# The last token tile's output columns cut 512 and 128 instead of 320 and 320, with a store for each part

## Chip, cores and metric

The kernel runs on one core of one Trainium2 chip. The metric is the device time of one execution in microseconds; the median of several executions is given, lower is better. Times inside an execution come from a hardware profile of one execution and are counted from the start of its span.

## What is computed

Input x has 2048 tokens of 640 channels in bf16. The output is the sum of x itself, a sliding-window attention on the layer-normalised x, and a gated bilinear unit on the same normalised x:

```
xn  = layernorm(x)
qkv = xn @ wqkv                                  # 32 heads of 20 channels
attn over 8 keys per token, 2 tokens apart       # masked at the start
a   = (attention output) @ wo
h   = (xn @ w_gate) * (xn @ w_up)                # 1536 wide
out = x + a + h @ w_down
```

The last line is the part that matters here. For 128 tokens and a group of output columns, `h @ w_down` (12 matmuls over the 1536 channels of h) and `o @ wo` (5 matmuls over the 640 channels of the attention output) are accumulated in the same PSUM bank, and x is added when the bank is read.

## The kernel before

The 2048 tokens are 16 tiles of 128 (`NT`), in 4 chunks of 4 tiles (`CH`). For each chunk the kernel runs the attention (`prodlog`, `softmax`, `av`: mostly VectorE, with short matmuls at line 484), the gated unit (`glu`: 24 groups of five 512-column matmuls at line 610, copied out by ScalarE at line 615 and multiplied by VectorE at line 626 into `hT`), then `down` for each of its four tiles, and between these the layer norm, transposes and projections of a later chunk (`ln`, `transposes`, `qk`, `vproj`). The last chunk has no later chunk beside it, so the end of the kernel is `glu` of chunk 3 and then `down(12)` to `down(15)`.

`down(t)` does the last line of the reference for one tile. `load_xr` fetches the tile of x into `xr` (a DMA on GpSimd's queue, long before). The 640 output columns are cut into two parts `n` of `NS` = 320 columns. For each part `pe` issues 12 matmuls of line 648 (weights: a 128x128 block of `hT`; moving: 320 columns of `wd`) and 5 of line 651 (weights: a block of the transposed attention output `oT`; moving: 320 columns of `wo`), all into one PSUM bank. `evict` then adds `xr` to the bank on VectorE (line 657) and writes the sum back into the same columns of `xr`. When both parts are done, `st` stores all 640 columns of the tile with one DMA (line 679): on GpSimd's queue for tiles 0 to 13, on SyncE's queue (SP) for tiles 14 and 15. For the first tile of a chunk (`q == 0`) the matmuls come in another order; tile 15 has `q == 3` and takes the plain branch.

The order of all instructions is made ahead of time by a planner (`Plan`). Every step is added with its engine, an estimated cost, how long it occupies the engine (`occ`), and the steps it depends on. `order` works out for each step the latest time at which it may start, counted back from the end over its successors' costs, and then runs through time: on each engine, of the steps that are ready, the one with the earliest such time goes first. The estimates decide the order only; on the chip each instruction starts when its engine and its semaphores allow. TensorE's main steps are chained by `pe_main`, which also lets a step wait for the eviction of the bank used six groups earlier (`ring`). Estimates that are used by `down` are 0.136 us for a matmul of 320 columns, 0.486 for an eviction and 2.3 for a store.

At the end of the program (line 794) SP waits for the semaphores of all DMAs and engines, two to an instruction, before the engines meet in a barrier.

Of the kernel before, what the change touches and what calls it, by code (L numbers as in the profile page):

```python
# [10 lines left out]
ALU = mybir.AluOpType  # L11
# [20 lines left out]
class Plan:  # L32
# [8 lines left out]
    def add(self, eng, cost, fn, deps=(), occ=None, after=(), kb=0):  # L41
        s = Step(eng, cost, fn, deps, occ, after)
        s.kb = kb
        s.idx = len(self.steps)
        self.steps.append(s)
        return s
# [51 lines left out]
def kernel(  # L98
# [11 lines left out]
    nc = tc.nc  # L110
    P = nc.NUM_PARTITIONS
    x_flat = A_x.flatten_outer_dims()
    out_flat = out.flatten_outer_dims()
    S, D = x_flat.shape
# [8 lines left out]
    KT = D // P  # L123
    FT = F // P
    NT = S // P
# [4 lines left out]
    NS = D // 2  # L130
# [12 lines left out]
    wo = const.tile([P, KT, D], BF, name="wo")  # L143
    wg = const.tile([P, KT, F], BF, name="wg")
    wu = const.tile([P, KT, F], BF, name="wu")
    wd = const.tile([P, FT, D], BF, name="wd")
# [7 lines left out]
    add = plan.add  # L154
    T = {}

    def new(key, shape, dtype, tag, bufs, pool=None):
        t = (pool or sb).tile(shape, dtype, name=tag, tag=tag, bufs=bufs)
        T[key] = t
        return t  # L160
# [127 lines left out]
    def st_in(t, g, d=None):  # L288
        return inline("DVE", 0.48, ln_stats(t, g), [d or X[t]], 0.395)
# [19 lines left out]
    def pe_main(cost, fn, deps=(), banks=1):  # L309
        nonlocal main  # L310
        waits = []
        for k in range(banks):
            if len(ring) + k >= 6:
                waits.append(ring[len(ring) + k - 6])
        main = add("PE", cost + 0.165, fn, [main, *waits, *deps], occ=cost)
        return main
# [313 lines left out]
    XR, OB = {}, {}  # L630

    def load_xr(t):
        def fn():
            x = new(("xr", t), [P, D], BF, "xr", 4)
            nc.gpsimd.dma_start(out=x[:], in_=x_flat[t * P : (t + 1) * P, :])
        XR[t] = add("POOL", 2.6, fn, [OB.get(t - 4), VS[6]], occ=0.5, after=[HT[t // CH, 3 + t % CH]])

    def down(t):
        c, q = divmod(t, CH)
        load_xr(t)  # L640
        evs = []
        def pe(n, f0, f1, wo_part):
            if f0 == 0:
                new(("psD", t, n), [P, 512], F32, "ps", 6, psum)
            ps = T["psD", t, n]
            sl = slice(n * NS, (n + 1) * NS)
            for f in range(f0, f1):
                nc.tensor.matmul(ps[:, 0:NS], lhsT=T["hT", c, f][:, q * P : (q + 1) * P], rhs=wd[:, f, sl],  # L648
                                 start=(f == 0), stop=(f == FT - 1 and not wo_part))
            for g in range(KT if wo_part else 0):  # L650
                nc.tensor.matmul(ps[:, 0:NS], lhsT=T["oT", t][:, g, :], rhs=wo[:, g, sl],  # L651
                                 start=False, stop=(g == KT - 1 and f1 == FT))

        def evict(n, a):
            def ev():
                sl = slice(n * NS, (n + 1) * NS)
                nc.vector.tensor_tensor(T["xr", t][:, sl], T["psD", t, n][:, 0:NS], T["xr", t][:, sl], ALU.add)  # L657
            e = add("DVE", 0.486, ev, [a, XR[t]], occ=0.4)
            ring.append(e)
            evs.append(e)  # L660

        hs = [HT[c, f] for f in range(FT)]
        W2 = [OE[t], WL["d"], WL["o"]]
        if q == 0:
            cut = FT - 2
            for n in range(2):
                pe_main((cut + KT) * 0.136, lambda n=n: pe(n, 0, cut, True), [*hs[:cut], *W2], banks=n + 1)
            ends = [pe_main(2 * 0.136, lambda n=n: pe(n, cut, FT, False), hs[cut:], banks=0) for n in range(2)]
            for n in range(2):
                evict(n, ends[n])  # L670
            a = ends[1]
        else:
            for n in range(2):
                a = pe_main((FT + KT) * 0.136, lambda n=n: pe(n, 0, FT, True), [*hs, *W2])
                evict(n, a)
        DT[t] = a

        def st():
            (nc.sync if t >= NT - 2 else nc.gpsimd).dma_start(out=out_flat[t * P : (t + 1) * P, :], in_=T["xr", t][:])  # L679

        OB[t] = add("SP" if t >= NT - 2 else "POOL", 2.3, st, evs, occ=0.5)


    a = st_in(0, 0)
    a = st_in(0, 1, a)
# [5 lines left out]
    a = st_in(1, 0)  # L691
    a = st_in(1, 1, a)
# [7 lines left out]
    a = st_in(2, 0)  # L700
    apply_in(1)
    transposes(1)
    a = st_in(2, 1, a)
# [3 lines left out]
    a = st_in(3, 0)  # L707
    a = st_in(3, 1, a)
# [48 lines left out]
    for c in range(NCH):  # L757
        attention(c)
        glu(c)
        between(c + 2, lambda q: down(c * CH + q))  # L760
        if c + 2 < NCH:
            halo(c + 2)
            qk(c + 2, 0, CS)
            for q in range(CH):
                vproj((c + 2) * CH + q)
# [33 lines left out]
```

## Time and profile before

| | |
|---|---|
| median of 3 runs | 267.35 us (267.27 to 267.51) |
| the profiled execution | 267.32 us, its span 265.6 us |
| TensorE clock granted, mean | 0.998 |
| matmuls of line 648 (320 columns) | 384, 57.4 us busy, 300 ns each |
| matmuls of line 651 (320 columns) | 160, 27.0 us busy, 299 ns each |
| matmuls of line 610 (512 columns) | 480, 119.4 us busy, 380 ns each |
| evictions of line 657 | 32, 14.8 us busy |
| stores of line 679, GpSimd's queue | 14 of 160 KB, 2.2 us from issue to landing |
| stores of line 679, SP's queue | 2 of 160 KB, 1.8 us from issue to landing |

The span runs from the first instruction to the last; the execution's own time is 1.7 us longer. Matmuls overlap each other in the array, so a matmul of 300 ns can follow another after 136 ns: the distance from start to start, not the duration, sets how long a row of them takes. "PEld" is the loading of weights, which runs beside the matmuls. "SPq" is SyncE's instruction queue, which issues DMAs. In a group's row, the number behind the bar is the busy time, then the mean duration, then the idle time of the engine before these instructions.

### The profile page before, as it was taken

The numbers are of one execution on the slowest core, as the hardware profiler recorded it, in microseconds if no ns is written. First come the engines' busy times: TensorE is split into PE (matmuls) and PEld (weight loads), VectorE is DVE, ScalarE is ACT, GpSimd is POOL, SyncE is SP. The second block draws the span as 40 slices with busy tenths as digits, with TensorE's granted clock in tenths as the row PEclk, the third lists the DMA queues.
The fourth block names the chain that finished last, engine by engine and source line by source line (L and its number), as shares of the span: only waits on it lengthen the run. The fifth ranks groups of instructions, "written<-read, shape, count | busy, mean of one in ns | idle before, by whom it ended". The sixth has DMA issues, their size and how long they took to land.

```text
span 265.6 us, 4131 instructions
## 1 busy us (share of the span) xinstructions
PE 260.1 (98%) x1594; PEld 141.5 (53%) x1594; DVE 215.5 (81%) x338; ACT 108.2 (41%) x200; POOL 40.7 (15%) x84
## 2 busy tenths in 40 slices
PE   7999999999999999999999999999999999999994
PEld 2645455444577546444466754644447764445772
DVE  5784999999999999999992999999829999921221
ACT  2666564655400166555510135555552005554000
POOL 4641025200021311400000100420000113000000
PEclk9999999999999999999999999999999999999999
DMA  7999998957496391993136937594129279110001
GB/s 224 375 406 390 368 205 263 295 137 222 113 239 144 74 367 59 299 307 32 25 71 97 334 136 222 144 288 41 20 71 346 67 230 151 25 25 0 27 33 41
DMA packets 47875, 45.89 MB, mean 173 GB/s; under 512 B 21954, under 2 KB 45008, under 8 KB 47856
## 3 DMA queue, kind: packets, MB, share of 16 engines
q1 hardware_dynamic: 43440, 35.95, 48.4%
q0 software_dynamic: 2384, 8.05, 9.7%
q10 hardware_dynamic: 2032, 1.64, 1.9%
q8 instruction: 12, 0.20, 0.4%
q14 instruction: 7, 0.06, 0.1%
HBM read 35.39 MB, written 5.26 MB: 153 GB/s over the span
## 4 chain that ended last, share of the span: by engine, by line
PE 95%; DVE 2%; DMA 1%; issue 0%
PE ps L610 39%; PE ps L648 20%; PE ps L403 16%; PE ps L651 8%; PE ps L436 7%; PE pl L484 4%; DVE st L251 1%; DMA x<-in_A_x_dram 1%; PE ps L345 0%; PE ps L331 0%; DVE x L270 0%; DVE xr L657 0%; DVE mv L257 0%; DVE ve L259 0%; DVE xnT L351 0%
## 5 line engine op out<-in xcount | busy, mean ns | idle before, releaser
L610 PE MATMUL ps<-xnT,wg 128*128 128x512 bf16 x240 | 59.7, 380 | 0.0
L610 PE MATMUL ps<-xnT,wu 128*128 128x512 bf16 x240 | 59.7, 380 | 0.0
L648 PE MATMUL ps<-wd,hT 128*128 128x320 bf16 x384 | 57.4, 300 | 0.0
L474 DVE TENSOR_TENSOR pw<-q,k 128x2560 bf16<-128x2560 bf16 x32 | 46.4, 1486 | 3.2 <-ACT k L410 3.0
L648 PEld LDWEIGHTS <-hT 128*128 128x128 bf16 x384 | 37.4, 98 | 15.9 <-issue 0.8
L571 DVE TENSOR_TENSOR v<-v,a 128x5120 bf16<-128x5120 bf16 x16 | 45.1, 2818 | 0.1
L615 ACT CAST gs<-ps 128x512 bf16<-128x512 f32 x48 | 28.1, 585 | 40.2 <-PE ps L610 40.2
L610 PEld LDWEIGHTS <-wu 128*128 128x128 bf16 x240 | 23.3, 98 | 28.7 <-issue 0.8
L610 PEld LDWEIGHTS <-wg 128*128 128x128 bf16 x240 | 23.3, 98 | 28.1 <-issue 0.8
L615 ACT CAST us<-ps 128x512 bf16<-128x512 f32 x48 | 28.1, 585 | 23.3 <-PE ps L610 22.3
L626 DVE TENSOR_TENSOR hT<-gs,us 128x512 bf16<-128x512 bf16 x48 | 19.8, 420 | 14.4 <-ACT us L615 14.3
L657 DVE TENSOR_TENSOR xr<-ps,xr 128x320 bf16<-128x320 f32 x32 | 14.8, 486 | 19.4 <-PE ps L651 15.6
L651 PE MATMUL ps<-wo,oT 128*128 128x320 bf16 x160 | 27.0, 299 | 0.0
L679 POOL DMA_DIRECT2D out_dram<-xr x14 | 7.6, 546 | 122.7 <-DVE xr L657 122.7
L580 DVE TENSOR_TENSOR v<-v 128x2560 bf16<-128x2560 bf16 x16 | 23.8, 1485 | 0.1
L436 PE MATMUL ps<-wv,xnT 128*128 128x320 bf16 x160 | 23.2, 300 | 0.4 <-ACT xnT L351 0.4
L403 PE MATMUL ps<-xnT,wk 128*128 128x512 bf16 x100 | 22.4, 380 | 0.0
L403 PE MATMUL ps<-xnT,wq 128*128 128x512 bf16 x100 | 22.2, 379 | 0.0
L436 PEld LDWEIGHTS <-xnT 128*128 128x128 bf16 x160 | 15.2, 98 | 7.2 <-ACT xnT L351 0.5
L651 PEld LDWEIGHTS <-oT 128*128 128x128 bf16 x160 | 15.6, 98 | 6.1
L410 ACT CAST q<-ps 128x512 bf16<-128x512 f32 x20 | 11.7, 585 | 16.7 <-PE ps L403 16.7
L497 ACT CAST L<-pl 128x512 bf16<-128x512 f32 x8 | 4.7, 585 | 29.2 <-PE pl L484 26.4
(58 smaller groups left out, 193.1 us busy)
## 6 DMA issues: line engine op xcount, KB each, us to landing
v<-vD SPq DMA_DIRECT2D x16, 1280.0 KB, 7.0
vD<-v_t POOLq DMA_DIRECT2D x16, 160.0 KB, 4.6
xr<-in_A_x_dram POOLq DMA_DIRECT2D x16, 160.0 KB, 5.9
out_dram<-xr POOLq DMA_DIRECT2D x14, 160.0 KB, 2.2
wg<-in_B_w_gate_dram SPq DMA_DIRECT2D x1, 1920.0 KB, 11.2
wu<-in_B_w_up_dram SPq DMA_DIRECT2D x1, 1920.0 KB, 16.5
wd<-in_B_w_down_dram SPq DMA_DIRECT2D x1, 1920.0 KB, 22.0
x<-in_A_x_dram SPq DMA_DIRECT2D x8, 160.0 KB, 4.5
```

What stands on the lines that cost most here:

```text
L403: nc.tensor.matmul(T[key][:, 0:n], lhsT=(wk if r else wq)[:, i, j * P : (j + 1) * P], rhs=T["xnT", c][:, i, lo : lo + n], start=(i == 0), ...
L410: nc.scalar.copy(dst, T[key][:, 0:n])
L436: nc.tensor.matmul(T["psv", t, n][:, 0:NS], lhsT=T["xnT", c][:, i, q * P : (q + 1) * P], rhs=wv[:, i, n * NS : (n + 1) * NS], start=(i == ...
L474: nc.vector.tensor_tensor(p[:], T["q", c][:], T["k", c][:, :, DIL * i : DIL * i + CS], ALU.mult)
L571: nc.vector.tensor_tensor(v[:].rearrange("p w (j h) -> p w j h", j=Dh, h=H), v[:].rearrange("p w (j h) -> p w j h", j=Dh, h=H), T["a", n][ ...
L580: nc.vector.tensor_tensor(v[:, 0:4, :], v[:, 0:4, :], v[:, 4:8, :], ALU.add)
L610: nc.tensor.matmul(ps[:], lhsT=(wu if r else wg)[:, i, f * P : (f + 1) * P], rhs=T["xnT", c][:, i, :], start=(i == 0), stop=(i == KT - 1))
L615: nc.scalar.copy(s[:], T[key][:])
L626: nc.vector.tensor_tensor(h[:], T["gs", c, f][:], T["us", c, f][:], ALU.mult)
L648: nc.tensor.matmul(ps[:, 0:NS], lhsT=T["hT", c, f][:, q * P : (q + 1) * P], rhs=wd[:, f, sl], start=(f == 0), stop=(f == FT - 1 and not wo ...
L651: nc.tensor.matmul(ps[:, 0:NS], lhsT=T["oT", t][:, g, :], rhs=wo[:, g, sl], start=False, stop=(g == KT - 1 and f1 == FT))
L657: nc.vector.tensor_tensor(T["xr", t][:, sl], T["psD", t, n][:, 0:NS], T["xr", t][:, sl], ALU.add)
```

## The change

For tile 15 alone the two parts are of 512 and 128 columns, and each part gets its own store on SP's queue as soon as its own eviction is done. The other tiles keep two parts of 320 and their one store. The estimates for matmuls and evictions are now formulas of the width, and these apply to all tiles; for 320 columns they come out slightly above the old constants. The old single estimate of 2.3 us for the store becomes 2.1 for each of the two.

```diff
+        last = t == NT - 1
+        at = [0, 512, D] if last else [0, NS, D]
+
         def pe(n, f0, f1, wo_part):
             if f0 == 0:
                 new(("psD", t, n), [P, 512], F32, "ps", 6, psum)
-            ps = T["psD", t, n]
-            sl = slice(n * NS, (n + 1) * NS)
+            sl = slice(at[n], at[n + 1])
+            ps = T["psD", t, n][:, 0 : at[n + 1] - at[n]]
             for f in range(f0, f1):
-                nc.tensor.matmul(ps[:, 0:NS], lhsT=T["hT", c, f][:, q * P : (q + 1) * P], rhs=wd[:, f, sl],
+                nc.tensor.matmul(ps, lhsT=T["hT", c, f][:, q * P : (q + 1) * P], rhs=wd[:, f, sl],
                                  start=(f == 0), stop=(f == FT - 1 and not wo_part))
             for g in range(KT if wo_part else 0):
-                nc.tensor.matmul(ps[:, 0:NS], lhsT=T["oT", t][:, g, :], rhs=wo[:, g, sl],
+                nc.tensor.matmul(ps, lhsT=T["oT", t][:, g, :], rhs=wo[:, g, sl],
                                  start=False, stop=(g == KT - 1 and f1 == FT))
 
         def evict(n, a):
             def ev():
-                sl = slice(n * NS, (n + 1) * NS)
-                nc.vector.tensor_tensor(T["xr", t][:, sl], T["psD", t, n][:, 0:NS], T["xr", t][:, sl], ALU.add)
-            e = add("DVE", 0.486, ev, [a, XR[t]], occ=0.4)
+                w = at[n + 1] - at[n]
+                sl = slice(at[n], at[n + 1])
+                nc.vector.tensor_tensor(T["xr", t][:, sl], T["psD", t, n][:, 0:w], T["xr", t][:, sl], ALU.add)
+            cost = 0.153 + (at[n + 1] - at[n]) / 960
+            e = add("DVE", cost, ev, [a, XR[t]], occ=cost - 0.08)
             ring.append(e)
             evs.append(e)
...
             for n in range(2):
-                a = pe_main((FT + KT) * 0.136, lambda n=n: pe(n, 0, FT, True), [*hs, *W2])
+                a = pe_main((FT + KT) * ((at[n + 1] - at[n]) / 2400 + 0.003), lambda n=n: pe(n, 0, FT, True), [*hs, *W2])
                 evict(n, a)
         DT[t] = a
 
-        def st():
-            (nc.sync if t >= NT - 2 else nc.gpsimd).dma_start(out=out_flat[t * P : (t + 1) * P, :], in_=T["xr", t][:])
-
-        OB[t] = add("SP" if t >= NT - 2 else "POOL", 2.3, st, evs, occ=0.5)
+        def st(lo=0, hi=D):
+            e = nc.sync if t >= NT - 2 else nc.gpsimd
+            e.dma_start(out=out_flat[t * P : (t + 1) * P, lo:hi], in_=T["xr", t][:, lo:hi])
+
+        if last:
+            for n in range(2):
+                add("SP", 2.1, lambda n=n: st(at[n], at[n + 1]), [evs[n]], occ=0.5)
+        else:
+            OB[t] = add("SP" if t >= NT - 2 else "POOL", 2.3, st, evs, occ=0.5)
```

## The prediction

> **What bounds the kernel now.** I read the page's totals first, then the chain that ended last, then the timeline and short windows of the last 6 us.
>
> ```profile
> span 265.6 us, 4131 instructions
> PE 260.1 (98%) x1594; PEld 141.5 (53%) x1594; DVE 215.5 (81%) x338; ACT 108.2 (41%) x200; POOL 40.7 (15%) x84
> ...
> PE 95%; DVE 2%; DMA 1%; issue 0%
> ```
>
> TensorE is busy for 98% of the span and holds 95% of the chain. So a change at the last tile can act in two ways only: through TensorE's own time, or through what follows TensorE's last matmul and has no cover. The end of the timeline shows the second:
>
> ```profile
> 259.50 1.79 PE L648 MATMUL ps<-wd,hT 128*128 128x320 bf16 x12
> ...
> 261.13 0.84 PE L651 MATMUL ps<-wo,oT 128*128 128x320 bf16 x5
> 262.01 0.49 DVE L657 TENSOR_TENSOR xr<-ps,xr 128x320 bf16<-128x320 f32 x1 [1.82 <-PE ps L651]
> 262.53 0.35 SPq L679 DMA_DIRECT2D out_dram<-xr  x1
> ```
>
> The last matmul ends at 261.13+0.84 = 261.97. The second eviction runs from 262.01 to 262.50, and the one store is issued at 262.53. The windows behind it (length, busy time of five engines, clock, DMA share, GB/s) split the rest:
>
> ```profile
> 262.53:263.38 0.85, 0.00 (x0) 0.00 (x0) 0.00 (x0) 0.00 (x0) 0.00 (x0) 1.00 0.00 0
> 263.38:263.98 0.60, 0.00 (x0) 0.00 (x0) 0.00 (x0) 0.00 (x0) 0.00 (x0) 1.00 0.77 273
> 263.98:264.34 0.36, 0.00 (x0) 0.00 (x0) 0.00 (x0) 0.00 (x0) 0.00 (x0) 1.00 0.00 0
> 264.34:265.60 1.26, 0.00 (x0) 0.00 (x0) 0.00 (x0) 0.00 (x0) 0.00 (x0) 0.61 0.00 0
> ```
>
> 0.85 us from issue to the first packet, 0.60 of packets, 0.36 until the landing releases SP, and 1.26 of closing work. The uncovered tail is 265.60-261.97 = 3.63 us, and of it only the eviction (0.49), the packets (0.60) and a little of the closing depend on how the tile is cut.
>
> **TensorE's part.** Removed: 34 matmuls of 320 columns; added: 17 of 512 and 17 of 128. Pitches (start to start): 320 columns, 1.63/12 = 0.136 us in the chain's rows of L648; 512 columns, 25.90/120 = 0.2158 in the chain's L610 row. For 128 columns the trace has the transposes of line 331, which load a new 128x128 weight for every matmul as lines 648 and 651 do:
>
> ```profile
> 17.27 0.72 PE L331 MATMUL ps<-ident,x 128*128 128x128 bf16 x10
> ```
>
> ```profile
> 17.06 0.76 PEld L331 LDWEIGHTS <-x 128*128 128x128 bf16 x10
> ```
>
> One such matmul takes 0.22, so ten of them have a pitch of (0.72-0.22)/9 = 0.0556, and their weight loads keep the pace though each lasts 98 ns: two are in flight. Tile 15 starts its first matmul at 259.50-17x0.136 = 257.19. After: the second part starts at 257.19+17x0.2158 = 260.86, its last matmul at 260.86+16x0.0556 = 261.75, and ends 0.22 later at 261.97. Before it was 261.97. TensorE gains nothing and loses nothing. Both ends for the pitch: 0.0556 (from the row) and 0.098 (loads strictly one after another), which is 17x0.042 = +0.72; a load and then the 0.056 stream behind it would be 0.154, +1.67. I take the row, since it is the same form of instruction.
>
> The Trainium skill speaks against this: "TensorE: Matmul & The Clock Gate", section Back-to-back issue gap, gives about 81 ns per matmul for sustained pairs of weight load and 128-column matmul. The trace's ten in a row ran at 56 ns. By the page's figure the second part would cost 17x0.025 = 0.43 us more, an estimate of about 267.2 for the whole.
>
> **Evictions.** These rows (busy us, mean ns) price the three widths:
>
> ```profile
> L657 DVE TENSOR_TENSOR xr<-ps,xr 128x320 bf16<-128x320 f32 x32 | 14.8, 486 | 19.4 <-PE ps L651 15.6 <-PE ps L648 3.8
> ...
> L541 DVE TENSOR_TENSOR a<-d,s 128x512 bf16<-128x512 f32 x8 | 5.5, 692 | 0.3
> ...
> L537 DVE TENSOR_TENSOR s<-s 128x128 f32<-128x128 f32 x8 | 2.3, 292 | 0.3
> ```
>
> The first eviction grows from 0.49 to 0.69. Its last matmul starts at 257.19+16x0.2158 = 260.64 and ends 0.38 later at 261.02, so it runs from 261.06 to 261.75, under the second part's matmuls (end 261.97): free, with 0.26 to spare before VectorE is wanted at 262.01. Were the second part's cover gone, it would cost up to 0.69. The second eviction shrinks from 0.49 to 0.29: 262.01 to 262.30, **-0.20** on the path. Bounds: 0.168 for the 14-column add on PSUM at line 496 and 0.486 for 320 columns give a line with 0.287 at 128, so between -0.19 and -0.21.
>
> **Stores.** One SP issue becomes two; SP has nothing else left. The first store (128 rows of 1024 B) is issued at 261.78 and SP is free again at 261.78+0.35 = 262.13; the second is due at 262.33, so it waits for nothing. Without those 0.20 us of slack each 0.1 of longer issue would count in full. The first store's packets run from 261.78+0.85 = 262.63 on. Each of 16 DMA engines moves 8 rows; packet records have a median of 55 ns for 1280 B, 32 ns for 640 B and 18 ns for 256 B, so 1024 B is about 46 ns, 8 of them 0.37, and with the 0.14 by which the engines started apart (0.60 less 8x55 and the completion packet) it ends at 263.14. The second starts at 262.33+0.85 = 263.18, just behind it. Its 8 packets of 256 B take 8x18 instead of 8x55 ns: **-0.30**. The 18 ns come from DMA transposes, not from a store to DRAM, which the trace doesn't show at this size; the slow end of the same records (95th percentile) is 35 ns, which leaves -0.16, and as slow as the 1280 B packets leaves 0. A gain beyond -0.30 is bounded by packets at no time at all, -0.44. I take 18 because it lies on the line through 640 and 1280 B. The first store lands at 263.14+0.36 = 263.50, before the second's 263.18+0.30+0.36 = 263.84; it ends nothing.
>
> On the same point the skill's "DMA: Bandwidth & Descriptors", section Specifications, says that writes under 512 B are done as read-modify-write and miss line rate; no row here shows such a store.
>
> **Closing.** After the landing SP runs through waits on other semaphores, some 0.06 us each (264.34, 264.41, 264.47 and so on to 264.71 in its record). The stores of tiles 14 and 15 complete on semaphores 101 and 102; SP's DMAs take eight in turn, and 104 comes next and is waited on right behind 102. A third store moves the last landing one wait later, with one wait fewer behind it: **-0.06**. If the order differs, 0 or +0.06.
>
> **Planner.** Costs written in the code shift for every tile: 17x(320/2400+0.003) = 2.318 instead of 2.312 a part, and 0.4863 instead of 0.486 an eviction. No instruction lasts longer for it, but over the 22 parts that run before tile 15 the planned TensorE time drifts by 0.13 us, and two steps that stand this close on an engine can change places. Cover: line 610's rows show 0.0 idle before TensorE, and line 617 needs a product of line 626 only three units (3x2.16 us) later, so one 1.49 us step of line 580 in front of it is normally absorbed. I take 0; without that cover it is +1.49.
>
> **Sum.** 0.00-0.20-0.30-0.06 = -0.56. The profiled execution took 267.32 us around its 265.6 us span, 0.03 under the median of 267.35. So 267.35-0.56 = **266.8**.
>
> **Rivals.** (1) *The small store keeps its price, or the narrow matmuls some of theirs.* With 35 ns packets and no closing gain 267.35-0.20-0.16 = 267.0; with 55 ns ones 267.15; with half of the +0.72 on top of the full gain 267.15. For it: no store of 256 B rows is in the trace. Against: the packet line above and the transposes. (2) *The second eviction waits for the first store.* Both touch the tile xr, the one writes columns 512 to 639, the other reads 0 to 511; if the order is kept by tile rather than by region, the eviction can't start before the first store lands. That store releases at 261.78+0.85+0.51+0.36 = 263.50 instead of 262.01, +1.49, and the sum is 267.35-0.56+1.49 = **268.3**, slower. It decides as soon as that wait exists: anything over 0.56+0.53 us of it is slower. Against: at line 345 the transposes of the first 384 columns of x start at 5.62 while the second part of line 270 still writes the other columns until 5.82, and line 436 reads the first half of wv at 6.53 while the second half lands at 7.57. Both are reads beside writes of other columns; a write beside a DMA's read isn't shown. (3) *Weight loads and streams take turns in the second part*: +1.67-0.56, **268.5**; it decides above a pitch of 0.056+1.09/17 = 0.12. The transposes are against it. A planner flip whose 1.49 us isn't absorbed gives 268.3 too. (4) *It doesn't do what it says*: the first store's landing ends last, as with 35 ns packets in both; then 267.1 or so.
>
> **Numbers.** Forecast 0.58 (own range 266.6 to 267.0); rival (1) 0.26; (2) 0.07; (3) with the flip 0.06; (4) 0.03. A measurement of this kernel tells about 0.2%, 0.53 us, from no change, so faster means under 266.82: 0.48 of the forecast's chance lies there, and 0.02 of rival (1). Same: 0.10+0.24+0.03 = 0.37. Slower, over 267.88: 0.13. The range 266.5 to 267.6 leaves out rivals (2) and (3) and a little at each end.
>
> **What would show it.** The last matmul ending within 0.05 of 261.97, with 128-column matmuls at 56 ns; the second eviction at 0.29 us, 0.04 after that end; two SP issues 0.5 us apart; packets of 256 B over 0.3 us; an end near 265.04. An eviction of line 657 released by a DMA would prove rival (2), a pitch over 0.06 rival (3), idle time on line 610 the planner's.

## The result, and the profile after

| | before | changed |
|---|---|---|
| median of 15 runs | 267.38 us (267.27 to 267.54) | 266.82 us (266.72 to 267.00) |
| ratio to before | | 0.9979, 95% interval 0.9972 to 0.9986 |
| span of the profiled execution | 265.59 us | 265.02 us |
| end of TensorE's last matmul | 261.98 us | 261.95 us |
| from there to the end of the span | 3.61 us | 3.07 us |

The kernel is 0.56 us faster, or 0.21%. The interval lies wholly below 1 and has the prediction's bound of 0.2% inside it, so the sign is settled and the side of that bound isn't. In the two profiles 0.55 of the span's 0.57 us lie behind TensorE's last matmul. The page's totals and its chain by engine are as before but for the length:

```profile
span 265.0 us, 4114 instructions
PE 259.1 (98%) x1575; PEld 141.0 (53%) x1594; DVE 215.5 (81%) x338; ACT 108.3 (41%) x200; POOL 40.6 (15%) x84
...
PE 95%; DVE 2%; DMA 1%; issue 0%
```

PEld counts 1594 weight loads as before, so no matmul was dropped: the 19 fewer under PE (1575) are records that the trace misses, 13 of them in line 610's group. The end of the changed kernel's timeline (start, length, engine, line, operation; lines 648, 651, 657 and 679 of before are now 651, 654, 661 and 685):

```profile
259.76 1.24 PE L654 MATMUL ps<-wo,oT 128*128 128x512 bf16 x5
...
260.84 0.83 PE L651 MATMUL ps<-wd,hT 128*128 128x128 bf16 x12
261.04 0.69 DVE L661 TENSOR_TENSOR xr<-ps,xr 128x512 bf16<-128x512 f32 x1 [3.18 <-PE ps L654]
...
261.51 0.44 PE L654 MATMUL ps<-wo,oT 128*128 128x128 bf16 x5
261.76 0.88 SPq L685 DMA_DIRECT2D out_dram<-xr  x2
261.99 0.29 DVE L661 TENSOR_TENSOR xr<-ps,xr 128x128 bf16<-128x128 f32 x1 [0.26 <-PE ps L654]
```

The 512-column eviction runs wholly under the 128-column matmuls and leaves VectorE 0.26 us idle before the last one. That idle time ends with a matmul, not with a DMA. To see where the 0.55 us went, the tail is cut at the same three events in both profiles: TensorE's end, the issue of the last store, and SP's release by its landing. The columns are length, five engines' busy time, clock, DMA share and GB/s. Before:

```profile
261.98:262.53 0.55, 0.00 (x0) 0.00 (x0) 0.49 (x1) 0.00 (x0) 0.00 (x0) 1.00 0.00 0
262.53:264.34 1.81, 0.00 (x0) 0.00 (x0) 0.00 (x0) 0.00 (x0) 0.00 (x0) 1.00 0.26 91
264.34:265.59 1.25, 0.00 (x0) 0.00 (x0) 0.00 (x0) 0.00 (x0) 0.00 (x0) 0.61 0.00 0
```

After:

```profile
261.95:262.31 0.36, 0.00 (x1) 0.00 (x0) 0.29 (x1) 0.00 (x0) 0.00 (x0) 1.00 0.00 0
262.31:263.82 1.51, 0.00 (x0) 0.00 (x0) 0.00 (x0) 0.00 (x0) 0.00 (x0) 1.00 0.37 109
263.82:265.02 1.20, 0.00 (x0) 0.00 (x0) 0.00 (x0) 0.00 (x0) 0.00 (x0) 0.79 0.00 0
```

The eviction gives 0.19, the last store 0.30, the closing 0.05. (The closing is what SP and the other engines still do once the last landing has released SP.)

### The profile page after: what moved, and what is told of

It is laid out like the page before. It is cut to its first block, busy times and chain, and to the rows that moved or that the text cites. A ratio compares the mean times of both kernels' runs of the same rounds, so it can differ in the third digit from the quotient of the medians.

```text
span 265.0 us, 4114 instructions
## 1 busy us (share of the span) xinstructions
PE 259.1 (98%) x1575; PEld 141.0 (53%) x1594; DVE 215.5 (81%) x338; ACT 108.3 (41%) x200; POOL 40.6 (15%) x84
## 4 chain that ended last, share of the span: by engine, by line
PE 95%; DVE 2%; DMA 1%; issue 0%
PE ps L610 39%; PE ps L651 20%; PE ps L403 16%; PE ps L654 8%; PE ps L436 7%; PE pl L484 4%; DVE st L251 1%; DMA x<-in_A_x_dram 1%; PE ps L345 0%; PE ps L331 0%; DVE x L270 0%; DVE mv L257 0%; DVE ve L259 0%; DVE xnT L351 0%; DVE xr L661 0%
## 5 line engine op out<-in xcount | busy, mean ns | idle before, releaser
L610 PE MATMUL ps<-xnT,wg 128*128 128x512 bf16 x227 | 59.0, 379 | 0.7
L651 PE MATMUL ps<-wd,hT 128*128 128x320 bf16 (+2 forms) x383 | 57.4, 299 | 0.1
L661 DVE TENSOR_TENSOR xr<-ps,xr 128x320 bf16<-128x320 f32 (+2 forms) x32 | 14.8, 484 | 19.2 <-PE ps L654 15.4
L654 PE MATMUL ps<-wo,oT 128*128 128x320 bf16 (+2 forms) x160 | 27.0, 299 | 0.0
```

The lines of the kernel that those rows point to most:

```text
L610: nc.tensor.matmul(ps[:], lhsT=(wu if r else wg)[:, i, f * P : (f + 1) * P], rhs=T["xnT", c][:, i, :], start=(i == 0), stop=(i == KT - 1))
L651: nc.tensor.matmul(ps, lhsT=T["hT", c, f][:, q * P : (q + 1) * P], rhs=wd[:, f, sl], start=(f == 0), stop=(f == FT - 1 and not wo_part))
L654: nc.tensor.matmul(ps, lhsT=T["oT", t][:, g, :], rhs=wo[:, g, sl], start=False, stop=(g == KT - 1 and f1 == FT))
```

## The experiments

The theory is the prediction's sum: what counts is the last part's eviction, the last store's packets, and the number of SP's waits behind its landing. Rivals put the gain elsewhere: A in storing in two pieces as such, B in the planner's new estimates and so in the body of the kernel, C in the narrow eviction alone, D in anything but the closing waits. Each edit is shown against the changed kernel. A span alone misleads here: TensorE's end moved between 261.89 and 262.45 us from profile to profile. So the table at the end of this section compares what comes after TensorE's end.

**The cut alone, one store.**

```diff
         if last:
-            for n in range(2):
-                add("SP", 2.1, lambda n=n: st(at[n], at[n + 1]), [evs[n]], occ=0.5)
+            add("SP", 2.1, st, evs, occ=0.5)
```

> The last tile keeps its parts of 512 and 128 columns but is stored by one DMA of 640 columns, after both evictions. Theory of the tail's sum: only the eviction's term is left, 0.29 us instead of 0.49 behind TensorE's end; packets of 1280 B again over 0.60 us, and the last store on semaphore 102 with one more wait behind it. 267.38-0.20 = 267.18, a span of 265.4. Rival A (all of the gain comes from storing in two pieces): 267.38, span 265.6. Rival B (the gain lies in the body of the kernel, by the planner's new estimates): as the changed kernel, 266.82.

Measured: 267.22 us, ratio 0.9994 (0.9985 to 1.0003). The interval holds the theory's 0.9993 and rival A's 1, so the time alone doesn't decide. The profile does; its windows at the three events:

```profile
262.45:262.81 0.36, 0.00 (x1) 0.00 (x0) 0.29 (x1) 0.00 (x0) 0.00 (x0) 1.00 0.00 0
262.81:264.61 1.80, 0.00 (x0) 0.00 (x0) 0.00 (x0) 0.00 (x0) 0.00 (x0) 1.00 0.26 91
264.61:265.86 1.25, 0.00 (x0) 0.00 (x0) 0.00 (x0) 0.00 (x0) 0.00 (x0) 0.75 0.00 0
```

The first window is that of the changed kernel, the other two those of the kernel before: the eviction's 0.19 is there and nothing else. Rival B falls with it, since all of the new estimates for matmuls and evictions are in this kernel. Its span of 265.9 instead of the expected 265.4 came at the other end of the kernel: from 9.3 us on, TensorE's weight loads run 0.48 later than in the profile of before, up to the last tile. Ahead of that, at line 436, TensorE waited 0.9 us for the load of wv, a wait that the profile of before doesn't have.

```profile
  DMA wv<-in_A_wqkv_dram: 0.9, 2
```

**The stores alone, cut 320 and 320.**

```diff
-        at = [0, 512, D] if last else [0, NS, D]
+        at = [0, NS, D]
```

> The last tile is cut 320 and 320 as before, each half stored on its own when its eviction is done. Theory of the tail's sum: eviction unchanged at 0.49; the last store has 8 packets of 640 B per engine, 32 ns each instead of 55, -0.18; one wait fewer behind the landing, -0.06; 267.38-0.24 = 267.14, a span of 265.4. Rival A (the gain is the two stores): 266.82. Rival C (only the narrow eviction counts): 267.38.

Measured: 267.14 us, ratio 0.9991 (0.9982 to 1.0000). After TensorE's end 3.37 us remain, 0.24 fewer than before: issue to release 1.63 instead of 1.81, closing 1.19 instead of 1.25, eviction unchanged. The packets' records have a median of 32 ns for 640 B. Rivals A and C both fall as full accounts. The two halves give 0.20 and 0.24 and not the whole 0.55, because the packets' gain grows as the last part narrows: 8 packets of 18 ns instead of 8 of 32 are the other 0.11.

**The parts in the other order.**

```diff
-        at = [0, 512, D] if last else [0, NS, D]
+        at = [0, 128, D] if last else [0, NS, D]
```

> The parts change places: 128 columns first, 512 last, each stored on its own. Theory of the tail's sum: TensorE ends at the same time; the last eviction takes 0.69 instead of 0.49, +0.20; the last store has packets of 1024 B, 47 ns instead of 55, 8 of them -0.06; closing -0.06; 267.38+0.08 = 267.46, span 265.7. Rival A (two stores, or the uneven cut as such, bring the gain): about 266.85. Rival of TensorE's side (narrow matmuls in the middle cost more than their 56 ns pitch): later than 267.5 with the last matmul's end moved by as much.

Measured: 267.50 us, ratio 1.0005 (0.9996 to 1.0014), and 3.68 us after TensorE's end, which came at 261.93, so the narrow matmuls in the middle cost nothing. The same cut with the same two stores gives nothing when the wide part comes last. This rules out that uneven parts or two stores help whatever the width of the last part.

**A middle cut.**

```diff
-        at = [0, 512, D] if last else [0, NS, D]
+        at = [0, 384, D] if last else [0, NS, D]
```

> The cut is moved to 384 and 256 columns, two stores. Theory of the tail's sum: the last eviction takes 0.42 (midway by columns between 0.29 at 128 and 0.49 at 320), -0.07; packets of 512 B, some 27 ns by the line through 256, 640 and 1280 B, 8x(55-27) = -0.22; closing -0.06; 267.38-0.35 = 267.03. Rival C (the eviction alone counts): 267.31. If the gain were a step at 128 columns and not a slope: 267.3 or above.

Measured: 266.99 us, ratio 0.9987 (0.9978 to 0.9996), 3.26 us after TensorE's end. The last eviction took 0.425 us and the 512 B packets 27 ns. It is a slope, not a step.

**Three parts.**

```diff
-        at = [0, 512, D] if last else [0, NS, D]
+        at = [0, 512, 576, D] if last else [0, NS, D]
...
-            for n in range(2):
+            for n in range(len(at) - 1):
                 a = pe_main(
...
-            for n in range(2):
+            for n in range(3):
                 add("SP", 2.1, lambda n=n: st(at[n], at[n + 1]), [evs[n]], occ=0.5)
```

> Three parts of 512, 64 and 64 columns, three stores. It asks how narrow a last part can be. Theory with a TensorE pitch that goes on falling with the columns (0.0286 us at 64): TensorE ends at the same time, the last eviction takes 0.22 instead of 0.29, but SP needs 0.40 from one store's issue to the next and the third store is issued at 262.56 instead of 262.31; packets of 128 B -0.04, one wait fewer -0.06; 266.96, span 265.1. Rival (weight loads hold the pitch at 0.056): TensorE ends 17x0.027x2 = 0.93 later, 267.6, span 265.8. If the loads of 98 ns can't overlap at this rate at all, 17x2x0.07 later, above 269.

Measured: 267.10 us, ratio 0.9990 (0.9981 to 0.9999). Its interval lies just below 1, and its median is 0.28 above the changed kernel's. Its timeline:

```profile
261.48 0.51 PE L651 MATMUL ps<-wd,hT 128*128 128x64 bf16 x12
...
261.83 0.31 PE L654 MATMUL ps<-wo,oT 128*128 128x64 bf16 x5
261.90 1.32 SPq L685 DMA_DIRECT2D out_dram<-xr  x3
262.17 0.22 DVE L661 TENSOR_TENSOR xr<-ps,xr 128x64 bf16<-128x64 f32 x1 [0.17 <-PE ps L654]
```

One 64-column matmul lasts 0.193 us, so twelve in 0.51 have a pitch of 0.029: weight loads of 98 ns keep up with that too, and the rival with the loads as the limit is out. The limit is SP. The three issues take from 261.90 to 263.22, and the last starts at 262.82 although its eviction ended at 262.40. The expected sum had SP at 0.40 from issue to issue; here it was 0.44 and 0.48. Cut at the same three events, this tail is 0.68, 1.51 and 1.14. Against the changed kernel the last issue came 0.32 later where 0.25 was expected, and from there to the release it took the same 1.51 where 0.04 less was expected: its packets ran for 0.23 instead of 0.27, but the first came 0.90 after the issue instead of 0.85. These 0.07 and 0.04 are most of the 0.14 us by which the run came out above its expectation. Three parts with two stores, which spares SP an issue, weren't tried.

**A second eviction that has to wait.** The first store covers one column of the second part, which the second store writes again.

```diff
-                add("SP", 2.1, lambda n=n: st(at[n], at[n + 1]), [evs[n]], occ=0.5)
+                add("SP", 2.1, lambda n=n: st(at[n], at[n + 1] + 1 - n), [evs[n]], occ=0.5)
```

> As the changed kernel, but the first store covers columns 0 to 512 instead of 0 to 511, one column of the second part; that column is stored again by the second store. The second eviction then has to wait until the first store has landed. This prices rival (2) of the prediction, the order kept by tile. Theory: the eviction starts at about 263.52 (the first store landed at 263.49 in the changed kernel) instead of 261.99, +1.53, all of it on the path: span 266.5, time 268.35. If something else behind TensorE covers it (the closing waits for another engine, say), less than +1.0.

Measured: 268.43 us, ratio 1.0042 (1.0028 to 1.0055). Its timeline shows the wait, now released by a DMA:

```profile
263.64 0.29 DVE L661 TENSOR_TENSOR xr<-ps,xr 128x128 bf16<-128x128 f32 x1 [1.88 <-DMA out_dram<-xr]
```

A single shared column costs 1.61 us against the changed kernel, and makes it slower than before. On SP the second store waits for the first too, but only until 263.57, and the eviction ends at 263.93; so the price is that of the eviction's wait. The run also shows that the program's semaphores keep order by region and not by tile: without the shared column the same instruction waits for TensorE alone.

**The estimates alone.** The last tile is cut and stored as before.

```diff
-        at = [0, 512, D] if last else [0, NS, D]
+        at = [0, NS, D]
...
-            for n in range(2):
-                add("SP", 2.1, lambda n=n: st(at[n], at[n + 1]), [evs[n]], occ=0.5)
+            add("SP", 2.3, st, evs, occ=0.5)
```

> Only the planner's estimates are those of the changed kernel; the last tile is cut 320 and 320 and stored by one DMA as before. Theory: nothing on the path changes, 267.38, and from TensorE's last end to the end of the span 3.61 us as before. Rival B (the new estimates bring part of the gain): below 267.2.

Measured: 267.48 us, ratio 1.0001 (0.9991 to 1.0010), 3.64 us after TensorE's end. In the profiles of before, of this run and of the changed kernel, each engine runs its instructions in the same order (for TensorE by its weight loads), but for the changed kernel's added store. Rival B is out.

**The closing waits, with the changed cut.** SP's DMAs take eight completion semaphores in turn, and SP waits for them in a fixed order at the end. Five more DMAs ahead of the last store move it to the end of that order.

```diff
+        elif t == NT - 2:
+            cut6 = [0, 112, 224, 336, 448, 544, D]
+            for n in range(6):
+                add("SP", 2.1, lambda n=n: st(cut6[n], cut6[n + 1]), evs, occ=0.5)
         else:
             OB[t] = add("SP" if t >= NT - 2 else "POOL", 2.3, st, evs, occ=0.5)
```

> As the changed kernel, but the store of tile 14 is cut into six DMAs by columns, all issued before TensorE ends, so that the last store's completion semaphore is the last of the eight in turn (110 instead of 104). Theory: SP's closing waits run in a fixed order at 0.06 us each, and five fewer of them lie behind the last landing: -0.30 against the changed kernel, 266.52, span 264.7. Rival D (the closing term is not on the path, because the other engines' barrier or the landing itself sets the end): 266.82, span 265.0. Should the six issues hold up the first store of tile 15, it shows as a second store later than 262.31.

Measured: 266.51 us, ratio 0.9968 (0.9955 to 0.9980). The windows of its profile at the three events:

```profile
262.20:262.56 0.36, 0.00 (x1) 0.00 (x0) 0.29 (x1) 0.00 (x0) 0.00 (x0) 1.00 0.00 0
262.56:264.04 1.48, 0.00 (x0) 0.00 (x0) 0.00 (x0) 0.00 (x0) 0.00 (x0) 1.00 0.37 111
264.04:264.93 0.89, 0.00 (x0) 0.00 (x0) 0.00 (x0) 0.00 (x0) 0.00 (x0) 1.00 0.00 0
```

The last window is 0.31 shorter than the changed kernel's 1.20, the other two are all but the same. SP had been free again since 259.9, so the added issues held up nothing. This version has the lowest median of all that were run, 0.31 us below the changed kernel's and 0.87 below before.

**The closing waits, with the cut of before.**

```diff
-        at = [0, 512, D] if last else [0, NS, D]
+        at = [0, NS, D]
...
-            for n in range(2):
-                add("SP", 2.1, lambda n=n: st(at[n], at[n + 1]), [evs[n]], occ=0.5)
+            add("SP", 2.3, st, evs, occ=0.5)
+        elif t == NT - 2:
+            cut7 = [0, 96, 192, 288, 384, 480, 560, D]
+            for n in range(7):
+                add("SP", 2.1, lambda n=n: st(cut7[n], cut7[n + 1]), evs, occ=0.5)
```

> As the kernel before (parts of 320 and 320, one store of tile 15), but the store of tile 14 is cut into seven DMAs, so that the store of tile 15 completes on the last of the eight semaphores (110 instead of 102). Theory: six of SP's closing waits, 0.06 us each, no longer lie behind the last landing, -0.37 with nothing else changed: 267.01, 3.24 us from TensorE's end to the end of the span. Rival: the closing saving in the run with tile 14 in six pieces came with the narrow last store and is absent here: 267.38.

Measured: 267.07 us, ratio 0.9987 (0.9978 to 0.9996). Its windows:

```profile
261.89:262.44 0.55, 0.00 (x0) 0.00 (x0) 0.49 (x1) 0.00 (x0) 0.00 (x0) 1.00 0.00 0
262.44:264.25 1.81, 0.00 (x0) 0.00 (x0) 0.00 (x0) 0.00 (x0) 0.00 (x0) 0.90 0.26 91
264.25:265.15 0.90, 0.00 (x0) 0.00 (x0) 0.00 (x0) 0.00 (x0) 0.00 (x0) 0.50 0.00 0
```

The first two windows are those of the kernel before to the hundredth, the third has lost 0.35. The closing term stands on its own, and rival D is out.

All runs by what comes after TensorE's last matmul, in us. "Expected" is 3.61 with the change that the expectation worked out against the kernel before, or 3.05 with that against the changed kernel. Beside these runs the kernel before had medians of 267.37 to 267.41:

| run | expected | measured | median |
|---|---|---|---|
| before | | 3.61 | 267.38 |
| changed | 3.05 | 3.07 | 266.82 |
| cut alone | 3.41 | 3.41 | 267.22 |
| stores alone | 3.37 | 3.37 | 267.14 |
| 384 and 256 | 3.26 | 3.26 | 266.99 |
| 128, then 512 | 3.69 | 3.68 | 267.50 |
| 512, 64, 64 | 3.19 | 3.33 | 267.10 |
| eviction waits for the store | 4.58 | 4.68 | 268.43 |
| tile 14 stored in six | 2.75 | 2.73 | 266.51 |
| estimates alone | 3.61 | 3.64 | 267.48 |
| cut of before, tile 14 stored in seven | 3.24 | 3.26 | 267.07 |

## Why the prediction was right

- **TensorE gains nothing.** Predicted end 261.97, measured 261.95; the second part's first matmul 260.84 instead of 260.86. Seventeen matmuls of 128 columns in a row kept the transposes' pitch: from the first at 260.84 to the last at 261.74, (261.74-260.84)/16 = 0.056.
- **Evictions.** 0.69 at 261.04 and 0.29 at 261.99, as worked out. The idle time ahead of the last one is the 0.26 that was to spare.
- **Stores.** The second was issued at 262.31 (262.33 predicted) and its packets ran from 263.15 to 263.42, 0.27 instead of the 0.30 in the sum. The term that was taken from DMA transposes is now measured: 256 B rows stored to DRAM have a median of 18 ns. SP was released at 263.82 (263.84). Two small misses cancel here: the packets gained 0.33 and not 0.30, and from the last packet to the release it took 0.40 instead of 0.36, which the sum had left as it was:

```profile
263.15:263.42 0.27, 0.00 (x0) 0.00 (x0) 0.00 (x0) 0.00 (x0) 0.00 (x0) 1.00 0.57 122
263.42:263.82 0.40, 0.00 (x0) 0.00 (x0) 0.00 (x0) 0.00 (x0) 0.00 (x0) 1.00 0.00 0
```

- **Closing.** 0.05 instead of 0.06. At this size the term could have been an accident of two profiles; the two runs that moved it by five and six waits made it 0.31 and 0.35.
- **Planner.** Taken at 0 and measured at 0.
- **Rivals.** (1) didn't happen: the small packets are as cheap as the line through the larger ones says. (2) is the one that would have turned the result. It didn't happen, because order is kept by region; the run with the shared column makes such a wait and prices it, at 1.61 instead of the 1.49 of the prediction, since the eviction started 0.09 after the first store's last completion, which the sum had at nothing, and that store landed a little later. (3) is out by a wide margin, at 64 columns too. (4) didn't happen: the first store released SP at 263.51, 0.31 before the second.

The sum was -0.56 and the medians moved by 0.56. The terms agree within 0.01 each, in the profiles; that the medians agree to the hundredth is luck, since the executions spread over 0.28 us and the store's term held two misses that cancel.

The Trainium skill's 81 ns per matmul at 128 columns ("TensorE: Matmul & The Clock Gate", section Back-to-back issue gap) isn't what this stretch showed. Here 17 in a row ran at 56 ns, behind matmuls of 512 columns that had gone on for 3.7 us. Whether a longer row would slow down wasn't tried.

## What to carry to other kernels

When one engine fills the span, price the end separately: what follows its last instruction is a serial chain of eviction, store and closing work, and here the first two links went by the size of the last piece. Make that piece as small as its own matmuls still hide the larger piece's eviction, here the 0.69 us of 512 columns under 0.96 us of matmuls, and stop when another link takes over, here SP when it had a third store to issue. The position of the last DMA's semaphore in the program's final waits is a link too, worth 0.06 us per wait in this kernel.

## What was not expected of the hardware

- Weight loads of 98 ns followed each other at the 29 ns pitch of 64-column matmuls, so by their records more than three were under way at once.
- An issue right behind another one took SP longer, with narrow rows and with wide ones. In the run with tile 14 in six, stores of 224 B rows took 0.36 and 0.33 us after a pause of SP, and 0.43 and 0.42 right behind another store. Loads of 1280 B rows at the start of the kernel before took 0.33 after a pause and 0.41 to 0.52 right behind another. So the 0.38 and 0.40 of the two stores of 128 B rows, each right behind another, don't show that narrow rows cost more to issue.
- Rows of 128 B, 256 B, 512 B, 640 B, 1024 B and 1280 B went to DRAM with medians of 13, 18, 27, 32, 47 and 56 ns a packet. There is no step below 512 B in the packets' own times.
